# Keep-warm matmuls with start times, later expected casts and two weight loads per slot in a fused attention kernel

## The chip, the cores and the metric

The kernel runs on one core of a Trainium2 chip. The metric is the device time of one execution in microseconds (us), as a median of several executions; lower is better. The engines have short names in the profile: PE is TensorE (matmuls and transposes), ACT is ScalarE (tanh, exp), DVE is VectorE, POOL is GpSimd, SP is SyncE, which issues transfers. Each engine runs its own queue in order, and engines wait for each other through semaphores.

## The reference

Two attention blocks run one after the other. The first has 8 batches of 12 heads with 448 tokens and a head dimension of 64, and caps its scores with a tanh. The second reads the first one's output as x of 448 x 768 per batch, projects it to q, k and v of 4 experts, runs causal attention for each expert, and weighs two of the four expert outputs per token by a gate.

```python
scores = cap * np.tanh(scale * np.matmul(q, k.transpose(0, 1, 3, 2)) / cap)
attn = softmax(scores); x = np.matmul(attn, v)      # heads side by side: 8 x 448 x 768
for e in range(4):
    a = softmax(causal(scale * (x @ wq[e]) @ (x @ wk[e]).T))
    out += gate[e] * (a @ (x @ wv[e]) @ wo[e])      # gate: softmax of the top 2 of x @ w_gate
```

## The kernel before

**Pairs and slots.** The 96 heads of the first block are worked as 48 pairs, six pairs to a batch. A pair p is loaded by SP in float32 (`load`, L294), cast to float16 (`a_cast`, L376: q at L385, k at L386, the last 64 rows of k at L391, then v in `a_castv`, L397), transposed on PE and copied to SBUF by DVE (`a_tr`, L408), multiplied on PE into scores (`fill`, L470), put through tanh on ACT (`tanh`, L489, the row at L510) and exp (`expo`, L512, the row at L516), and multiplied with v on PE (`a_pv`, L575, rows L544 and L550). A last transpose (`a_xt`, L622, row L585) lays the result out as the second block's x. Pairs 0 and 1 have their q cast by DVE; from pair 2 on every cast is POOL's.

The program on ACT is fixed: a list `prog` in which each pair has a slot. The tanh of a pair comes in four parts, written here T(p,0) to T(p,3), and from pair 3 on the exp of the pair before, E(p-1), stands between T(p,0) and T(p,1). The scores live in two buffers, so the fill of one part can begin only when ACT has read the part two places earlier. The second block's exps (L781, called X) come in between for the batches that are done; X of batch 0 stands in slots 9 and 11.

**Who orders PE's queue.** A `Plan` (L17 to L129) simulates PE, DVE and ACT while the kernel is built and so decides in which order the units of work are put into PE's queue. Its clock begins at 7.0. It knows `dur` (L998): a slot without second-block exps is 0.055 + 0.373, then three times 0.055 + 0.746, then 0.08 + 0.00084 x 3136, which is 5.545. `nom["S", p]` is the nominal start of slot p, counted from 0, so `nom + 7` is the planner's own time of it. A unit has a cost, dependencies, and a due time; it is a candidate once its dependencies are in `plan.done`. `step` (L64) takes, among the candidates that can start within 0.3 of the earliest, the one with the earliest due time. `do_fill` (L1019) places each fill at the time at which its buffer is expected to be free, and lets `pump` (L85) put units into the gap before it. The planner's times set the order alone. On the chip PE takes the next instruction in the queue as soon as the semaphores allow it.

**`slot(p)` (L1046)** is called when the program reaches slot p. It drops the keep-warm units left from the slot before and offers new ones; issues the loads of pairs six slots ahead; casts the pair four slots ahead (`a_cast`) and tells the planner when to expect that cast, in `plan.done[("cast", i)]`; issues some of the second block's weight loads from POOL's queue (L1064) and tells the planner to expect them 26.0 later; and offers the transposes of pair p + 2, the products of pair p - 1, and in slots 6, 12, ... the projections of a finished batch (`batch`, L1117). A cast and a weight load that are issued in the same slot stand behind each other in POOL's queue.

**Keep-warm units** (`keep_warm`, L894) are matmuls of a zero tile, 128 x 512, into a buffer that nothing reads. They have a due time of 1.0e9, so the planner takes one only where nothing else can start within 0.3. Nine and two more are issued before the planner begins.

There are 16 weight loads: q and k of experts 0 and 1 (four), v (four), q and k of experts 2 and 3 (four), and the output weights (four), in this order.

Of the kernel before, what the change touches and what calls it, by code (L numbers as in the profile page):

```python
# [239 lines left out]
def kernel(  # L240
# [15 lines left out]
    B, H, S, Dh = q.shape  # L256
# [37 lines left out]
    def load(p, n=2):  # L294

        b, j = divmod(p, HP)
        h0, h1 = 2 * j, 2 * (j + n)
        qf = stage.tile([QP, 2 * n, QC * Dh], f32, name=f"qf_{p}", tag="qf")
        kf = stage.tile([128, 2 * n, KC * Dh], f32, name=f"kf_{p}", tag="kf")
        vf = stage.tile([128, 2 * n, KC * Dh], f32, name=f"vf_{p}", tag="vf")  # L300
        ktf = stage.tile([128, n, Dh], f32, name=f"ktf_{p}", tag="ktf")
        vtf = stage.tile([128, n, Dh], f32, name=f"vtf_{p}", tag="vtf")
        for i in range(n):
            h = slice(2 * i, 2 * i + 2)
            staged[p + i] = (qf[:, h], kf[:, h], vf[:, h], ktf[:, i], vtf[:, i])

        def rows(dst, src, c):
            return lambda eng: eng.dma_start(dst, src.rearrange("h (p c) d -> p h (c d)", c=c))

        def tails(dst, src, i):  # L310
            t = src[b, h0:h1, KM:S].rearrange("(j two) p d -> two p j d", two=2)
            return lambda eng: eng.dma_start(dst[64 * i : 64 * (i + 1)], t[i])  # L312

        return [
            rows(qf, q[b, h0:h1], QC), rows(kf, k[b, h0:h1, 0:KM], KC), tails(ktf, k, 0),
            tails(ktf, k, 1), rows(vf, v[b, h0:h1, 0:KM], KC), tails(vtf, v, 0), tails(vtf, v, 1),
        ]
# [3 lines left out]
    LOAD, CAST, TR = 6, 4, 2  # L321
    DEEP = 18

    def ahead(p, n, since, more=4):

        new = range(p + n + more * (p > since), p + n + more * (p >= since) + 1)
        return [i for i in new if i < NP]

    warm = const.tile([128, 512], f16, name="warm")
# [46 lines left out]
    def a_cast(p):  # L376
        if p >= NP:
            return
        eng = nc.vector if p < 2 else nc.gpsimd
        assert p < 8 or ("tr", p - 8) in plan.done  # L380
        assert p < 12 or ("pv", p - 12, 1) in plan.done
        qf, kf, vf, ktf, vtf = staged.pop(p)
        q16 = hd.tile([QP, QC, 2, Dh], f16, name=f"q16_{p}", tag="q16", bufs=8)
        k16 = hd.tile([128, KC, 2, Dh], f16, name=f"k16_{p}", tag="k16", bufs=8)
        eng.tensor_copy(q16, qf.rearrange("p h (c d) -> p c h d", c=QC))  # L385
        nc.gpsimd.tensor_copy(  # L386
            k16, kf.rearrange("p h (c d) -> p c h d", c=KC)
        )
        for g in range(2):
            r = slice(64 * g, 64 * (g + 1))  # L390
            eng.tensor_copy(ktz[p % 8][r, r], ktf[r, :])  # L391
        cast[p] = (q16, k16)
        vcast[p] = (vf, vtf)
        if p > 1:
            a_castv(p)
# [506 lines left out]
    plan = Plan()  # L902
# [35 lines left out]
    def b_const(i):  # L938
        if i == 0:
            nc.gpsimd.memset(ltm, 0.0)  # L940
            nc.gpsimd.affine_select(
                out=ltm, in_=ltm, compare_op=ALU.is_ge, fill=-60000.0, base=0,
                pattern=[[1, 128]], channel_multiplier=-1,
            )
        else:
            nc.vector.memset(vtL, 0.0)
            nc.vector.memset(vtL[64:128, :, Dh : Dh + 1], 1.0)
        nc.vector.memset(vtB[i], 0.0)
        nc.vector.memset(vtB[i][0:64, 0:E:2, Dh : Dh + 1], 1.0)
        nc.vector.memset(vtB[i][64:128, 1:E:2, Dh : Dh + 1], 1.0)  # L950
        for t in pB[2 * i : 2 * i + 2]:
            nc.vector.memset(t[:, 0:64], 0.0)
# [85 lines left out]
    nom = {}  # L1038
# [7 lines left out]
    def slot(p):  # L1046

        plan.work[:] = [u for u in plan.work if u["key"][0] != "warm"]
        for i in range(14 if p < 3 else 8 if p < 7 else 4 if p < 13 else 0):
            plan.add(("warm", p, i), 0.22, 0.0, [], 1.0e9, keep_warm)  # L1050
        if p % 2 == 0:
            for i in ahead(p, LOAD, DEEP):
                if i % 2 == 0:
                    for f in load(i):
                        f(nc.sync)
        for i in ahead(p, CAST, DEEP + 2):
            a_cast(i)
            plan.done[("cast", i)] = max(
                5.0 * i + 1.0, plan.act + 4.0 + 3.5 * (i - p - CAST) * (p == DEEP + 2)
            )  # L1060
        for _ in range(3 if p else 2):
            if loads:
                w, dst, src = loads.pop(0)
                nc.gpsimd.dma_start(dst, src)  # L1064
                plan.done["w", w] = plan.act + 26.0
        if p in (4, 5):
            b_const(p - 4)
        for i in (1, 2) if p == 0 else ahead(p, TR, DEEP + 4, 4):
            plan.add(("tr", i), 0.43, 0.95, [("cast", i)], nom["S", i] - 3.0, a_tr, i)
        if 1 <= p < len(UNITS):  # L1070
            u = UNITS[p - 1]
            es = [("E", u)]
            due = nom["S", p + 1] + 2.0
            if isinstance(u, tuple):
                i = "AB".index(u[1])
                u = u[0]
                plan.parts(("pv", u, i), 2, 0.47, 0.55, es, due, a_pv, u, i)
                d = [("pv", u, i)]
                plan.add(("xt", u, "AB"[i]), 0.12, 0.27, d, due, a_xt_part, u, i)
            else:  # L1080
                plan.parts(("pv", u, 0), 2, 0.47, 0.55, es, due, a_pv, u, 0)
                d = [("pv", u, 0)]
                plan.parts(("pv", u, 1), 2, 0.47, 0.55, d, due, a_pv, u, 1)
                plan.add(("xt", u), 0.22, 0.35, [("pv", u, 1)], due, a_xt, u)
        if p >= HP and p % HP == 0 and p < NP:
            batch(p // HP - 1)
        if p == NP - 1:
            last_qk()
        if p == NP:
            last_vg()  # L1090
# [6 lines left out]
    def last_qk():  # L1097
        for r in range(2):
            g = ("qk", "A", r)
            due = nom["X", B - 1, r, 0] - 2.0  # L1100
            for j in range(NDC):
                d = [x_of(j, "A"), ("w", ("q", r)), ("w", ("k", r))] + [(*g, j - 1)] * (j > 0)
                plan.add(
                    (*g, j), 0.22, 0.66 * (j == NDC - 1), d, due, qk_mm, "A", r, j,
                    aux={0: "open", NDC - 1: "close"}.get(j), group=g,
                )

    def last_vg():

        due = nom["X", B - 1, 1, 0]  # L1110
        d = [x_of(NDC - 1, "A")]
        plan.parts(("vl", 0), 4, 1.32, 0.75, d, due, lv_part)
        plan.add(("lgA",), 0.6, 0.2, d, due, l_logits)
        plan.add(("g1A",), 0.0, 1.0, [("lgA",)], due, b_gate, B - 1, "A", aux=None)
        plan.add(("gA",), 0.0, 0.8, [("g1A",), ("G", B - 1)], due, b_gate2, B - 1, "A", aux=None)

    def batch(b):  # L1117
        x = ("xt", HP * b + HP - 1)
        t0, t1 = nom["X", b, 0, 0], nom["X", b, 1, 0]
        for r, t in enumerate((t0, t1)):  # L1120
            plan.parts(("q", b, r), 3, 1.13, 0.55, [x, ("w", ("q", r))], t - 4.0, b_qk, b, r, "q")
            plan.parts(("k", b, r), 3, 1.13, 0.55, [x, ("w", ("k", r))], t - 4.0, b_qk, b, r, "k")
        for n in range(4):
            d = [("v", b, n - 1)] if n else [x, ("w", "v")]
            plan.parts(("v", b, n), 2, 0.66, 0.6, d, t0 + 2.0 * n, b_v, b, n)
        plan.add(("g1", b), 0.0, 1.0, [("v", b, 3)], t1 + 1.0, b_gate, b, aux=None)
        plan.add(("g", b), 0.0, 0.8, [("g1", b), ("G", b)], t1 + 3.0, b_gate2, b, aux=None)
        for e in range(E):
            due = t1 + 6.0 + 3.0 * e
            d = [("X", b, e // 2, 1), ("g", b)] + [("pvB", b, e - 1)] * (e % 2)  # L1130
            plan.add(("pvB", b, e), 0.31, 0.7, d, due, b_pv, b, e)
            if e % 2:
                plan.add(("oT", b, e // 2), 0.22, 0.35, [("pvB", b, e)], due, b_ot, b, e // 2)
        for n in range(4):
            for f in range(2):
                i = 2 * n + f
                d = [("oT", b, 1), ("w", "o")] if i == 0 else [("wo", b, *divmod(i - 1, 2))]
                due = t1 + 19.0 + 1.5 * i
                plan.add(("wo", b, n, f), 0.33, 0.5, d, due, b_wo, b, n, f)
# [522 lines left out]
```

## Time and profile before

| what | value |
|---|---|
| median of 5 runs | 324.2 us (323.09 to 325.06) |
| the profiled execution's own time | 324.7 us |
| span of its profile, first to last instruction | 323.0 us |
| outside the span | 1.7 us |
| ACT busy | 306.2 us, 95% of the span |
| PE busy | 287.4 us, 89% |
| DVE busy | 217.8 us, 67% |
| POOL busy (its DMA issues are not counted) | 157.2 us, 49% |
| mean granted PE clock | 0.993 |
| keep-warm matmuls in the trace | 82 |

The table is read from the profile's page and the dummy tile's rows. A busy share is an average over the whole span. What bounds a stretch is read from that stretch: the row that stood idle there, and the engine named as releaser. In a timeline row the first two numbers are the start and the length of a group of like instructions, `x7` is how many there are, and the bracket at the end is the engine's idle time just before the group with the row that ended it. Lengths of PE rows overlap, since matmuls are pipelined; the distance between starts tells more.

### The profile page before, as it was taken

The page shows a single profiled execution, that of the slowest core. Times are in us where ns is not written, and L with a number is a line of the kernel's source. Part 1 is how long each engine was busy: PE and PEld are TensorE (multiplying, and loading weights), DVE is VectorE, ACT ScalarE, POOL GpSimd, SP SyncE. Part 2 cuts the span into 40 slices and gives each one's busy share as a digit, 9 for nine tenths or more (in the row PEclk, how much of TensorE's full clock was granted, in tenths as well). Part 3 has the DMA queues.
Part 4 walks back from the last instruction along what each step waited for, and adds up shares of the span by engine and source line. Part 5 has one row for each costly group of instructions (what it writes and reads, how often), then busy time and mean ns, then how long its engine had stood idle before and what let it go on. Part 6 is the DMA issues. An engine that isn't in the chain of part 4 may idle for free.

```text
span 323.0 us, 9113 instructions
## 1 busy us (share of the span) xinstructions
PE 287.4 (89%) x3454; PEld 179.9 (56%) x3454; DVE 217.8 (67%) x760; ACT 306.2 (95%) x311; POOL 157.2 (49%) x480
## 2 busy tenths in 40 slices
PE   7879899998999789997899889997899879999991
PEld 2445556654565555665555655655565555557760
DVE  4434446776767777678766985777867975578672
ACT  3996999999999999999999999999999999999881
POOL 3639999865806389874914386082804200220200
PEclk9997999999999999999999999999999999999999
DMA  7599999990185989786073990279012102020027
GB/s 158 166 222 248 221 231 230 234 205 3 50 220 145 254 212 287 184 218 151 11 212 127 284 227 2 101 197 217 4 52 97 26 2 98 2 76 2 3 99 244
DMA packets 65404, 46.22 MB, mean 143 GB/s; under 512 B 26000, under 2 KB 61968, under 8 KB 65360
## 3 DMA queue, kind: packets, MB, share of 16 engines
q1 hardware_dynamic: 54000, 43.19, 51.9%
q0 software_dynamic: 10512, 1.58, 7.2%
q10 hardware_dynamic: 848, 0.87, 0.8%
q8 instruction: 27, 0.44, 0.6%
q14 instruction: 17, 0.14, 0.1%
HBM read 36.19 MB, written 11.01 MB: 146 GB/s over the span
## 4 chain that ended last, share of the span: by engine, by line
ACT 73%; PE 12%; issue 6%; DMA 5%; SPq 1%; DVE 1%; POOL 1%; POOLq 0%
ACT y L510 34%; ACT p L516 28%; ACT pBs L781 8%; DMA qf<-in_q_dram 4%; DMA kf<-in_k_dram 2%; PE wops L863 2%; PE vps L640 1%; PE pv L550 1%; PE dummy L898 1%; PE qkA L1163 1%; ACT pB L516 1%; SPq L312 1%; PE pv L544 1%; PE kps L724 1%; ACT yB L510 1%
## 5 line engine op out<-in xcount | busy, mean ns | idle before, releaser
L510 ACT ACTIVATE y<-s 128x896 f16<-128x896 f32 (+1 forms) x176 | 140.6, 973 | 3.2 <-PE s L480 2.7
L516 ACT ACTIVATE p<-y 128x3136 f16<-128x3136 f16 x44 | 130.7, 2970 | 0.1
L789 POOL TENSOR_SCALAR_AFFINE_SELECT pBs<-pBs 128x128 f16<-128x128 f16 (+1 forms) x112 | 28.3, 278 | 106.6 <-ACT pBs L781 104.8
L550 PE MATMUL pv<-v16s,p 128*128 128x65 f16 x1056 | 54.6, 194 | 0.0
L480 PE MATMUL s<-qt,kt 64*128 64x448 f16 x264 | 46.6, 356 | 7.8 <-ACT y L510 5.2
L550 PEld LDWEIGHTS <-p 128*128 128x128 f16 x1056 | 46.8, 98 | 3.4 <-issue 0.3
L544 PE MATMUL pv<-vtzs,p 128*128 128x130 f16 x176 | 39.5, 224 | 8.3 <-ACT p L516 6.0
L563 DVE TENSOR_TENSOR xk<-pv,rc 128x256 f16<-128x256 f32 x96 | 40.7, 424 | 3.3
L559 DVE RECIPROCAL rc<-pv 128x4 f32<-128x4 f32 x96 | 17.2, 179 | 33.2 <-PE pv L550 31.6
L370 DVE COPY ob<-wops 128x384 f32<-128x384 f32 (+1 forms) x53 | 29.3, 553 | 9.4 <-PE wops L863 9.1
L544 PEld LDWEIGHTS <-p 128*128 128x128 f16 x176 | 17.1, 97 | 27.2 <-ACT p L516 16.3
L480 PEld LDWEIGHTS <-kt 64*128 64x128 f16 x264 | 16.4, 93 | 28.2 <-issue 20.6
L781 ACT ACTIVATE pBs<-sB 128x960 f16<-128x960 f32 (+1 forms) x28 | 32.1, 1162 | 0.0
L385 POOL CAST q<-qf 112x512 f16<-112x512 f32 x46 | 28.1, 611 | 6.3 <-DMA qf<-in_q_dram 4.4
L863 PE MATMUL wops<-wo,oT 128*128 128x384 f16 x128 | 29.9, 326 | 0.3 <-ACT oT L370 0.3
L640 PE MATMUL vps<-wvg,xT 128*128 128x260 f16 (+1 forms) x192 | 29.8, 275 | 0.0
L399 POOL CAST v16s<-vf 128x384 f16<-128x384 f32 x48 | 24.3, 506 | 6.0 <-DMA vf<-in_v_dram 3.2
L370 DVE COPY xT<-xtp 128x448 f16<-128x448 f16 (+2 forms) x52 | 19.1, 368 | 11.5 <-PE xtp L585 10.1
L386 POOL CAST k<-kf 128x384 f16<-128x384 f32 x48 | 24.3, 506 | 3.9 <-DMA kf<-in_k_dram 3.9
L898 PE MATMUL dummy<-warm 128*128 128x512 f16 x82 | 24.9, 422 | 1.3 <-DVE warm L330 1.3
L404 POOL CAST vtzs<-vtf 64x64 f16<-64x64 f32 x96 | 22.6, 235 | 3.4 <-DMA vtf<-in_v_dram 0.6
L391 POOL CAST ktzs<-ktf 64x64 f16<-64x64 f32 x92 | 21.3, 232 | 2.8
(178 smaller groups left out, 527.4 us busy)
## 6 DMA issues: line engine op xcount, KB each, us to landing
qf<-in_q_dram SPq DMA_DIRECT2D x22, 448.0 KB, 6.0
out_dram<-ob SPq DMA_DIRECT2D x23, 384.0 KB, 2.5
kf<-in_k_dram SPq DMA_DIRECT2D x22, 384.0 KB, 6.8
vf<-in_v_dram SPq DMA_DIRECT2D x22, 384.0 KB, 6.0
ktf<-in_k_dram SPq DMA_DIRECT2D x44, 32.0 KB, 5.7
vtf<-in_v_dram SPq DMA_DIRECT2D x44, 32.0 KB, 5.2
out_dram<-ob SPq DMA_DIRECT2D x7, 192.0 KB, 2.8
kf<-in_k_dram SPq DMA_DIRECT2D x4, 192.0 KB, 3.3
```

The lines of the kernel that those rows point to most:

```text
L370: (nc.scalar.copy if act else nc.vector.tensor_copy)(dst, src)
L480: nc.tensor.matmul(sc[:, g, 0:S], kt[r, 128 * i : 128 * (i + 1)], qt[r, :], start=True, stop=True,)
L510: nc.scalar.activation(dst, src, AF.Tanh, scale=isc / capf)
L516: nc.scalar.activation(pt[:, 0:n], y.pop(u)[:, 0:n], AF.Exp, scale=capf)
L544: nc.tensor.matmul(pv[:, n, :, :], prob(p, w, 0, 0), vtz[p % 12], start=(n == 0), stop=False, skip_group_check=True,)
L550: nc.tensor.matmul(pv[:, n, g, :], prob(p, w, j, g), v16[p % 12][:, g, j - 1, :], start=False, stop=(j == KC), skip_group_check=True,)
L563: nc.vector.tensor_tensor(xt[p][:, 2 * i : 2 * i + 2, :, :], pv[:, :, :, 0:Dh], rc.broadcast_to((128, 2, 2, Dh)), ALU.mult,)
L640: nc.tensor.matmul(ps, xT[b][:, j, w : w + 128], wvg[:, j, 0 : ps.shape[1]], start=(j == 0 and first), stop=(j == NDC - 1), skip_group_che ...
L781: nc.scalar.activation(pb[:, o0 : o0 + n], st[b].pop(("sc", r, g))[:, 0:n], AF.Exp, scale=isc)
L789: nc.gpsimd.affine_select(out=blk, in_=blk, compare_op=ALU.is_ge, fill=0.0, base=0, pattern=[[1, n]], channel_multiplier=-1,)
L863: nc.tensor.matmul(ps, st[b]["oT", r][:, w : w + 128], wo2[r][:, f * (D // 2) : (f + 1) * (D // 2)], start=(r == 0), stop=(r == 1),)
L898: nc.tensor.matmul(dummy, warm[:, 0:128], warm, start=True, stop=True)
```

## The change

Three edits are made in `slot`, and nothing else changes.

```diff
     def slot(p):
 
         plan.work[:] = [u for u in plan.work if u["key"][0] != "warm"]
-        for i in range(14 if p < 3 else 8 if p < 7 else 4 if p < 13 else 0):
-            plan.add(("warm", p, i), 0.22, 0.0, [], 1.0e9, keep_warm)
+        n = 9 if p < 3 else 6 if p < 7 else 3 if p < 13 else 0
+        for i in range(n):
+            plan.done["from", p, i] = nom["S", p] + 7.0 + 5.6 * i / n
+            plan.add(("warm", p, i), 0.22, 0.0, [("from", p, i)], 1.0e9, keep_warm)
...
         for i in ahead(p, CAST, DEEP + 2):
             a_cast(i)
             plan.done[("cast", i)] = max(
-                5.0 * i + 1.0, plan.act + 4.0 + 3.5 * (i - p - CAST) * (p == DEEP + 2)
-            )
-        for _ in range(3 if p else 2):
+                5.65 * i + 1.5 if i < 12 else 0.0,
+                plan.act + 4.0 + 3.5 * (i - p - CAST) * (p == DEEP + 2),
+            )
+        for _ in range(2):
             if loads:
                 w, dst, src = loads.pop(0)
                 nc.gpsimd.dma_start(dst, src)
                 plan.done["w", w] = plan.act + 26.0
```

First, fewer keep-warm units are offered (9, 6 and 3 in a slot in place of 14, 8 and 4), and each has a time before which the planner doesn't take it, spread evenly over 5.6 from the slot's start. Second, the planner expects the cast of pair i at 5.65 i + 1.5 in place of 5.0 i + 1.0 up to pair 11; from pair 12 on only the second term counts. Third, every slot issues at most two weight loads, so the 16 loads take slots 0 to 7 in place of 0 to 5.

## The prediction

> **What bounds the kernel now.** I read the page first, then ACT's waits, then ACT's, PE's and POOL's timelines around the longest wait, then a table of windows.
>
> The page, busy tenths in 40 slices of 8.1 us:
>
> ```profile
> PE   7879899998999789997899889997899879999991
> ACT  3996999999999999999999999999999999999881
> PEclk9997999999999999999999999999999999999999
> ```
>
> ACT is full from the second slice to the 37th, but for the fourth. There the granted PE clock also has its only dip. ACT's waits by releaser:
>
> ```profile
> ACT kt L370 <- PE tpsk L421: 2.8, 1, 2.8
> ACT y L510 <- PE s L480: 2.7, 1, 2.7
> ACT ob L370 <- PE wops L863: 2.4, 2, 1.9
> ```
>
> The first is the start (6.15 us), the third the end (after 305); neither place is edited. The second is one wait of 2.7 us. ACT around it:
>
> ```profile
> 24.64 1.75 ACT L510 ACTIVATE y<-s 128x896 f16<-128x896 f32 x2
> 29.11 1.35 ACT L510 ACTIVATE y<-s 128x896 f16<-128x896 f32 x2 [2.71 <-PE s L480]
> ```
>
> By its place in the program this is T(3,3), late by 2.71 us. PE's queue before it:
>
> ```profile
> 22.02 0.37 PE L414 MATMUL tps<-ident,q 112*128 112x112 f16 x4 [0.30 <-POOL q L385]
> 23.70 0.23 PE L419 MATMUL tps<-ident,ktzs 128*128 128x128 f16 x1 [1.30 <-POOL ktzs L391]
> 24.02 0.55 PE L480 MATMUL s<-qt,kt 64*128 64x448 f16 x4
> ...
> 24.74 3.03 PE L898 MATMUL dummy<-warm 128*128 128x512 f16 x7
> 27.56 0.32 PE L544 MATMUL pv<-vtzs,p 128*128 128x130 f16 x1
> ...
> 28.70 0.36 PE L480 MATMUL s<-qt,kt 64*128 64x448 f16 x2
> ```
>
> PE takes up the transposes of pair 4 at 22.02 and stands until 23.70 for POOL's cast. Then come seven dummies, the products of pair 2, one more dummy, and only then the fill that ACT wants. The windows (columns: us, then busy time and count of PE, PEld, DVE, ACT, POOL; granted clock; DMA share; GB/s):
>
> ```profile
> 21.50:24.90 3.40, 1.80 (x24) 0.99 (x22) 1.38 (x5) 3.40 (x4) 1.96 (x6) 1.00 1.02 255
> 24.90:28.30 3.40, 3.40 (x20) 1.65 (x18) 0.41 (x2) 1.50 (x2) 3.24 (x8) 0.50 1.15 257
> 260.40:263.80 3.40, 2.16 (x29) 1.43 (x29) 3.03 (x12) 3.40 (x6) 0.00 (x0) 1.00 0.00 0
> ```
>
> After the thin stretch at 21.5 the clock is halved for one stretch of 3.4 us. A stretch with PE busy for 2.16 kept it.
>
> **Where the 2.71 come from.** Later, at full clock, eight dummies begin 1.89 us from first start to last end, and one alone takes 0.38: (1.89 - 0.38) / 7 = 0.216 apart. Seven are 1.51; here they took 27.56 - 24.74 = 2.82. The products took 28.39 - 27.56 = 0.83, and 0.50 at 33.22. The eighth dummy took 0.31, not 0.22. The clock so accounts for 1.31 + 0.33 + 0.09 = 1.7, and the stand with the dummies behind it for the other 1.0.
>
> **Part by part.**
>
> *Expected casts.* The planner took pair 4's cast for done at 5 x 4 + 1 = 21.0. E(2) stands at 21.35 in its clock (slot 3 is 7 + 2.83 + 2 x 5.545 = 20.92, and T(3,0) is 0.43) and at 21.94 in the trace, so the trace's clock is 0.6 later there. The cast ended in the trace at 23.12 + 0.52 = 23.64, that is 23.0 for the planner: two late. After the change it is expected at 5.65 x 4 + 1.5 = 24.1. By hand, the planner then puts the fills of T(3,1) and T(3,2) first (21.2 to 21.9), the output transposes of pair 1, four dummies that its start times allow (20.92, 21.85, 22.79, 23.72), pair 4's transposes at 24.1, pair 2's first products to 25.0, and the fill of T(3,3) at 25.01. On the chip: the cast is there at 23.64, the transposes end near 24.1; the products wait for E(2), to about 24.8, and end near 25.3; the fill's buffer is free when T(3,1) ends, 24.64 + 0.81 = 25.45; with the 0.41 from fill to ACT it is ready at 25.9. T(3,2) ends at 24.64 + 1.75 = 26.39 at the latest. The wait is gone, 2.7 us, with 0.4 to spare: **-2.7**. If the clock were halved all the same, the products (0.83) would end at 25.7 and the fill (about 0.7) at 26.4: a rest of 0.4. Bounds: 0 and -2.71; taken is the whole, since the rows leave room.
>
> What is late next? Pairs 5 to 11 are expected 0.105 later each relative to their slots (5.65 against 5.545). Pair 6's transposes move behind the dummies of slot 5: planned 35.4, copied by DVE at 37.2, wanted by T(6,0) at 37.6. For pairs 7 to 9 the planner's margin is slightly negative (-0.1 to -0.3). On the chip it isn't: POOL's casts of pair 5 ended at 28.5 and went on 5.0 apart, so PE finds them done and doesn't wait for the planned minute. By the 0.43 of the transposes and 0.95 of DVE's copies, pair 9 is ready near 53.4, wanted near 54.9. Cost taken: 0; bounds 0 to 0.3 in each of slots 7 to 9, so 0.9.
>
> *Keep-warm units.* In slots 0 to 2 the ones offered nearly cover the ones taken (two fewer in slot 0). In slot 3 four or five stand where one stood in the thin stretch: 1.80 + 3 x 0.22 is about 2.5 busy, above the 2.16 that kept the clock. In slots 4 to 6 five are taken in place of eight: 0.65 us less in 5.55. The stretch there with the fewest, 38.6 to 42.0, had PE busy for 3.07; if all three were lost in it 2.4 remain. Cost taken: 0, as PE has waits there; bounds -0.2 (less in front of a fill) and, per lost stretch, the 1.7 above.
>
> [...]
>
> *Two weight loads.* A load holds POOL's queue for 0.83 us. Slots 1 to 4 have issued three; with two, casts of pairs 6 to 9 come up to 2.5 us sooner, and the same loads delay pairs 10 to 13, which then end where they did, at 61.7. As ACT is 2.7 ahead, POOL's masks of batch 0 (first at 61.97, behind those casts) are no longer immediate, but their reader stands in PE's queue near 64. Cost 0, cover 2.
>
> The delicate place is the q and k weights of experts 2 and 3. Before, the last q load went at 41.16 and landed 17.8 us later, 58.9; PE used it at 60.23. Now it goes near 46.8, and PE comes to it near 59.5: the planner holds it back to 32.0 + 26 = 58.0 and places it at 58.75. The loads of that queue landed 1.3 to 3.3 us apart from 38.7 on whatever their spacing at issue, with four or more outstanding, so I expect the same landing, 58.9: cost 0. With the least, median and greatest latency of the loads issued after 38 us (13.0, 16.0, 17.8) it would land at 59.8, 62.8 or 64.6: PE would stand 0.3, 3.3 or 5.1 us, and ACT, with 0.4 of room, lose 0, 2.9 or 4.7.
>
> From slot 13 on no edit reaches the planner's inputs but through its state. ACT had no wait there from 29.11 to 305, so everything should move forward by the same 2.7.
>
> **Sum.** 324.7 - 2.7 = **322.0** against the profiled execution's own time. The median before is 324.2, 0.5 less; its fastest run, 323.09, is what my division gives without the halved clock (324.7 - 1.7 = 323.0), so I take the runs to differ in that wait, and 322.0 for the median too. Its own range is 321.2 to 322.6.
>
> **Rivals.**
> 1. *A part of the wait stays*: cast 4 depends on a DMA landing (k at 22.6), or the clock still falls. 0.4 to 1.7 remain: 322.4 to 323.7. For it: 0.4 of room only, one profile. Against: the dummies now lie where PE stood. Chance 0.18.
> 2. *The wait moves to the weights* in slot 9, landing at 62.8: -2.7 + 2.9, 324.9, no change. For it: latency grew to 17.8 with load. Against: the landings are paced by the queue. Chance 0.08. The end (PE and ACT after 290) reordered for the worse by 1 to 2 us gives the same time: 0.04.
> 3. *Slower: the same weights land later still.* From a landing past about 64.0 on, a loss of 4.3 or more puts it over 325.8; at 64.6 it is 326.7. Chance 0.10.
>
> **Numbers.** The forecast has 0.60. I call 0.5% (1.6 us) what a measurement of this kernel can tell from no change: faster is below 322.6, slower above 325.8. Faster: the forecast, 0.60 (what of it lies above that line, rival 1 makes up below it). Same: rivals 1 and 2, 0.30. Slower: rival 3, 0.10. The range leaves out rival 3 and the worst of 2: 321.1 to 324.6.
>
> **What the profile after would show.** Right: no ACT wait for s L480 near 26; four or five dummies between 22 and 23.7 and pair 4's transposes after them without a stand over 0.3 us; clock 1.00 through 40 us; ACT's last exp of a pair ending near 302.4, not 305.1. Wrong: a PE wait for a wq or wk landing near 60; a clock of 0.50 in slots 3 to 8; DVE's copies of pairs 6 to 9 followed by an ACT wait; or rows equal up to 290 and a longer end.

## The result and the profile after

| what | before | after |
|---|---|---|
| median | 325.13 us (79 runs, 323.09 to 329.37) | 326.72 us (44 runs, 324.14 to 330.04) |
| the profiled execution's own time | 324.7 us | 325.82 us |
| span of its profile | 323.0 us | 324.1 us |
| mean granted PE clock in the profile | 0.993 | 0.989 |
| keep-warm matmuls in the trace | 82 | 67 |

The ratio after to before is 1.0046, with a 95% interval of 1.0032 to 1.0060: slower by 1.0 to 2.0 us. That is just inside the 0.5% that the prediction called no change, and it lies 4.7 us above the forecast of 322.0 and above the whole range. Here and below, medians and ranges are of all runs, while ratios leave out the few slow ones, over 1.5% above the fastest run of their kernel.

The page of after, busy tenths in 40 slices of 8.1 us:

```profile
ACT  3999996999999999999999999999999999999882
PEclk9999999999999989999999999999999999999997
```

ACT's hole has moved, from the fourth slice to the seventh (48.6 to 56.7 us), and the clock's dip from the fourth (0.50 from 24.91 to 28.32) to the 15th (0.50 from 118.78 to 122.20; the 7 in the last slice lies behind ACT's work). ACT's longest waits, and PE's waits for a DMA:

```profile
ACT y L510 <- PE s L476: 4.1, 3, 3.0
ACT kt L370 <- PE tpsk L421: 2.9, 1, 2.9
ACT ob L370 <- PE wops L863: 2.4, 2, 1.9
```

```profile
PE vps L640 <- DMA wvg<-in_moe_wv_dram: 2.8, 1, 2.8
```

The wait of 2.7 for L480 is gone. In its place stands one of 3.0 for a fill at L476, and PE now waits 2.8 for the v weights (`wvg`), a row that the profile before doesn't have. First the place that was to be mended, PE's queue in slot 3 of after:

```profile
21.94 0.62 PE L480 MATMUL s<-qt,kt 64*128 64x448 f16 x4
...
22.73 1.03 PE L898 MATMUL dummy<-warm 128*128 128x512 f16 x4
23.59 0.36 PE L414 MATMUL tps<-ident,q 112*128 112x112 f16 x4
...
25.71 0.36 PE L480 MATMUL s<-qt,kt 64*128 64x448 f16 x2
```

The order is the one that the prediction worked out by hand: fills, four dummies, pair 4's transposes without a long stand, pair 2's products, and the fill of T(3,3) at 25.71 in place of 28.70. Then PE's queue in slots 7 and 8 of after, and behind it ACT's T(8,0), which waits for the row at 52.16:

```profile
48.51 0.54 PE L724 MATMUL qps<-xT,wq 128*128 128x448 f16 x2
51.82 0.51 PE L640 MATMUL vps<-wvg,xT 128*128 128x260 f16 x3 [2.77 <-DMA wvg<-in_moe_wv_dram]
52.16 0.35 PE L476 MATMUL s<-qt,kt 128*128 128x448 f16 x1
```

```profile
52.55 0.54 ACT L510 ACTIVATE y<-s 128x448 f16<-128x448 f32 x1 [3.03 <-PE s L476]
```

And the same place of before:

```profile
48.56 0.92 PE L724 MATMUL qps<-xT,wq 128*128 128x448 f16 x4
...
51.52 0.35 PE L476 MATMUL s<-qt,kt 128*128 128x448 f16 x1
...
54.39 0.83 PE L640 MATMUL vps<-wvg,xT 128*128 128x260 f16 x6
```

The last v load, its issue and then its row in the list of issues (KB and us to landing), before:

```profile
36.12 0.85 POOL L1064 DMA_DIRECT2D wvg<-in_moe_wv_dram  x1
```

```profile
wvg<-in_moe_wv_dram POOLq DMA_DIRECT2D x1, 96.0 KB, 13.9
```

And after:

```profile
39.15 0.83 POOL L1067 DMA_DIRECT2D wvg<-in_moe_wv_dram  x1
```

```profile
wvg<-in_moe_wv_dram POOLq DMA_DIRECT2D x1, 96.0 KB, 12.6
```

Before, PE first put all of q and k of batch 0 through and came to the v products at 54.39; the last v load had landed at 50.07. After, three v products stand between q's first part and the fill of T(8,0). PE reaches them at 48.9, the last v load lands at 51.77, and the fill behind them, which has nothing to do with the weights, comes 3.03 us late for ACT.

The spans add up: -2.71 (slot 3) + 3.03 (slot 8) + 0.64 (a wait of ACT at 121.96, at the end of the stretch at 0.50 from 118.78 on) + 0.14 (the first tanh begins at 7.33, before at 7.19) = +1.10, and 324.1 - 323.0 = 1.1.

**Why the v products come so early.** Working the planner through on paper, which needs only the kernel's text, gives this. It puts the first v product at 50.93 in before and at 48.28 in after. The reason is the edit of the expected casts alone: the transposes of pairs 7 and 8 are expected later and move back in the queue. Pair 7's now stand in front of pair 5's products, and the last output transpose that batch 0 lacks (`xT` of pair 5) is put at 45.41 in place of 44.34. Pair 8's now stand between it and the first part of batch 0's q, which is put at 47.91 in place of 45.31. So the gap in front of T(8,0)'s fill, which q's third part filled before, is now filled by the first v products. For the planner the v weights are there: the last v load is issued in slot 3 and expected 26.0 later, at 46.92. In the trace it landed at 51.77; the trace's clock is some 0.9 later than the planner's there, so it came 4 us later than planned. In before the same constant was off by more (expected at 41.4, landed at 50.07), but no product stood near enough to feel it.

### The profile page after: what moved, and what is told of

Read it like the earlier page. It is cut to its first block, busy times and chain, and to the rows that moved or that the text cites. A ratio compares the mean times of both kernels' runs of the same rounds, so it can differ in the third digit from the quotient of the medians.

```text
span 324.1 us, 9086 instructions
## 1 busy us (share of the span) xinstructions
PE 284.1 (88%) x3439; PEld 179.2 (55%) x3439; DVE 215.8 (67%) x760; ACT 306.4 (95%) x311; POOL 157.2 (48%) x480
## 4 chain that ended last, share of the span: by engine, by line
ACT 66%; PE 15%; issue 6%; DMA 6%; POOL 4%; DVE 1%; SPq 0%; POOLq 0%
ACT y L510 31%; ACT p L516 25%; ACT pBs L781 8%; DMA wvg<-in_moe_wv_dram 4%; PE wops L863 2%; PE vps L640 2%; DMA vf<-in_v_dram 2%; PE pv L550 1%; PE dummy L898 1%; PE qkA L1166 1%; ACT pB L516 1%; PE pv L544 1%; PE sB L762 1%; POOL v16s L399 1%; PE s L480 1%
## 5 line engine op out<-in xcount | busy, mean ns | idle before, releaser
L510 ACT ACTIVATE y<-s 128x896 f16<-128x896 f32 (+1 forms) x176 | 138.5, 934 | 4.2 <-PE s L476 4.1
L516 ACT ACTIVATE p<-y 128x3136 f16<-128x3136 f16 x44 | 128.8, 2928 | 0.1
L550 PE MATMUL pv<-v16s,p 128*128 128x65 f16 x1056 | 56.3, 194 | 0.0
L480 PE MATMUL s<-qt,kt 64*128 64x448 f16 x264 | 46.8, 358 | 9.7 <-ACT y L510 7.1
L550 PEld LDWEIGHTS <-p 128*128 128x128 f16 x1056 | 47.6, 98 | 3.9 <-issue 0.4
L544 PEld LDWEIGHTS <-p 128*128 128x128 f16 x176 | 17.1, 97 | 28.8 <-ACT p L516 15.8
L480 PEld LDWEIGHTS <-kt 64*128 64x128 f16 x264 | 16.1, 93 | 29.5 <-issue 22.9
L781 ACT ACTIVATE pBs<-sB 128x960 f16<-128x960 f32 (+1 forms) x28 | 30.6, 1110 | 0.0
L898 PE MATMUL dummy<-warm 128*128 128x512 f16 x67 | 21.9, 414 | 1.3 <-DVE warm L330 1.3
```

Of the source, the lines that this page charges most:

```text
L480: nc.tensor.matmul(sc[:, g, 0:S], kt[r, 128 * i : 128 * (i + 1)], qt[r, :], start=True, stop=True,)
L510: nc.scalar.activation(dst, src, AF.Tanh, scale=isc / capf)
L516: nc.scalar.activation(pt[:, 0:n], y.pop(u)[:, 0:n], AF.Exp, scale=capf)
L544: nc.tensor.matmul(pv[:, n, :, :], prob(p, w, 0, 0), vtz[p % 12], start=(n == 0), stop=False, skip_group_check=True,)
L550: nc.tensor.matmul(pv[:, n, g, :], prob(p, w, j, g), v16[p % 12][:, g, j - 1, :], start=False, stop=(j == KC), skip_group_check=True,)
L781: nc.scalar.activation(pb[:, o0 : o0 + n], st[b].pop(("sc", r, g))[:, 0:n], AF.Exp, scale=isc)
```

## The experiments

My theory A was this: all of the loss is the v weights, so with v expected later the change keeps its gain. Rival B: the thinner keep-warm matmuls cost clock (0.985 as a mean over the runs of after, 0.992 over those of before), and the stand for v (PE idle until the load lands) is only a part. Rival C: the two-load edit alone is to blame, since it sends the v loads out 3 us later.

**e1, the changed kernel with the weights expected later.**

```diff
-                plan.done["w", w] = plan.act + 26.0
+                plan.done["w", w] = plan.act + 31.0
```

> The changed kernel, but the planner expects each weight load 31.0 after its issue in place of 26.0; nothing else. Theory A (the changed kernel lost its gain to PE standing 2.77 us in front of the v weights, which landed at 51.77 while PE came at 48.9): the first v product moves from 48.3 to 53.7 of the planner's clock, about 54.5 of the trace's, behind the landing; the ACT wait of 3.03 us in slot 8 goes, the span is near 321 and the median 3 us under the changed kernel's 326.7, near 323.7, a ratio to before of 0.995. Rival B (what costs is the clock, which the fewer keep-warm matmuls let fall more often): the wait may go, but mean clocks stay near 0.985 and the median stays above 325.5, ratio 1.001 or more.

Measured: 322.60 us (321.89 to 323.29) against 324.55 of before; ratio 0.9937 (0.9912 to 0.9962). PE in slots 7 and 8 of e1:

```profile
48.52 0.54 PE L724 MATMUL qps<-xT,wq 128*128 128x448 f16 x2
48.90 0.38 PE L898 MATMUL dummy<-warm 128*128 128x512 f16 x1
49.12 0.35 PE L476 MATMUL s<-qt,kt 128*128 128x448 f16 x1
...
54.16 0.50 PE L640 MATMUL vps<-wvg,xT 128*128 128x260 f16 x3
```

A dummy takes the place of the v products, the fill goes at 49.12 in place of 52.16, and ACT has no wait at slot 8. One constant turns the change from +0.46% to -0.63%. A is carried; all three edits are still in e1, so the other two cost little. The median is 1.1 us below what A gave (323.7), which took only ACT's wait off; e9 to e12 are about the rest.

**e2, the expected casts alone** (before with the second edit only).

> The kernel before with the second edit alone: later expected casts, three weight loads per slot, old keep-warm units. Theory A: the 2.71 us wait in slot 3 goes; the planner puts the first v product at 48.3 here too, and with three loads per slot the v weights land near 50.1, so PE stands about 1.2 us and ACT waits about 1.4 in slot 8; the sum is -1.3, ratio 0.996. Rival B: the keep-warm units are the old ones, so all of the wait removed is gained unless the weights take it; ratio 0.992 to 0.996 and clocks no lower than before's.

Measured: 326.42 us (324.47 to 329.83); ratio 1.0057 (1.0021 to 1.0093). The expectation was missed: the edit that was to bring the gain loses by itself. The wait in slot 3 is gone in e2 too, but PE waits for weights twice:

```profile
PE qps L724 <- DMA wq<-in_moe_wq_dram: 1.6, 1, 1.6
PE vps L640 <- DMA wvg<-in_moe_wv_dram: 0.8, 1, 0.8
```

ACT loses 1.07 at 50.65 and 1.43 at 62.60 by them. C falls: with three loads per slot v lands at 49.87, and PE is there before it all the same.

**e3, the two weight loads alone** (before with the third edit only).

> The kernel before with the third edit alone: two weight loads per slot. Both theories: the 2.71 us wait in slot 3 stays, and the first v product stays at 50.9 of the planner's clock, some 54.4 of the trace's, behind a landing near 51.8, so nothing waits for weights: ratio 1.000, within 0.3%. If it is slower by 0.5%, the loads cost in a way that neither theory has.

Measured: 323.49 us (322.51 to 326.17); ratio 0.9968 (0.9940 to 0.9997). The wait in slot 3 is there (2.94 in its profile), and PE waits for no weight, though v lands at 50.72. Alone the edit costs nothing; why it is slightly faster, if it is, the profile doesn't show.

**e4, the keep-warm matmuls alone** (before with the first edit only).

> The kernel before with the first edit alone: fewer keep-warm units with start times. Theory A: four dummies in place of seven stand before the late fill of slot 3, so its wait shortens by 0.6 to 1.2 us and nothing else moves: ratio 0.997. Rival B: clocks fall more often, the mean clock is about 0.005 lower than in before's runs and the time longer by one or two lost stretches of some 0.7 to 1.7 us: ratio 1.003 to 1.008.

Measured: 324.38 us (322.81 to 326.66); ratio 1.0006 (0.9975 to 1.0037), and a mean clock of 0.992 as before. In its profile the wait in slot 3 is 0.36, since fewer dummies stand behind the transposes and the clock wasn't halved there (1.00 from 24.9 to 28.3, behind 3.40 us with PE busy for 1.85). But the next pairs have the same fault of order, a little later. PE and ACT around slot 6 of e4:

```profile
38.07 0.37 PE L414 MATMUL tps<-ident,q 112*128 112x112 f16 x4 [0.60 <-POOL q L385]
38.99 0.23 PE L419 MATMUL tps<-ident,ktzs 128*128 128x128 f16 x1 [0.55 <-POOL ktzs L391]
```

```profile
39.83 0.54 ACT L510 ACTIVATE y<-s 128x448 f16<-128x448 f32 x1 [1.16 <-PE s L476]
```

PE stands for POOL's cast again, in front of the fill of T(6,0). Without the later expected casts the wait moves; with them it goes.

**e5, the changed kernel with 28.0 in place of 26.0.** For the planner this moves the v products alone (to 53.66) and leaves the q and k weights of the later experts where they are.

> The changed kernel with the weights expected 28.0 after issue in place of 26.0: by the planner's arithmetic this moves the v products of batch 0 (first from 48.3 to 53.7) and leaves the q product of experts 2 and 3 at 60.0, so the v weights are the one wait taken away. Theory A: as e1 was, 322.6, ratio 0.994. If the q weights of experts 2 and 3 (landing 59.8 to 61.3, reached near 60.9) also cost in most executions, it stays 0.5 us or more above e1.

Measured: 322.42 us (322.23 to 322.95) against 324.70; ratio 0.9917 (0.9887 to 0.9948). No wait of ACT longer than 0.1 us between 8 and 304 us. So it is v, not q and k, that costs.

**e6, e1 with the old keep-warm units.**

> e1 with the old keep-warm units (14, 8, 4 and no start times). Theory A (with the weight wait gone the fewer keep-warm units cost nothing on ACT): 322.6 as e1, within 0.3%, whatever the clock. Rival B (the thinned units cost): faster than e1 by 0.5 us or more, 322.1 or less, with a mean clock of 0.992 as before's.

Measured: 321.61 us (321.25 to 323.14); ratio 0.9900 (0.9863 to 0.9938), the fastest of all, with a mean clock of 0.993. These are the numbers that were given for rival B, though e1 ran on another chip. Against e5, on the same chip, it is 0.8 lower, and the intervals overlap. The profiled executions differ by nearly as much (322.23 and 321.54), but not where the dummies stand: neither has a wait of ACT over 0.1 us between 8 and 304 us, the last copy to the output ends at 314.80 in e5 and at 314.71 in e6, and behind it, where the output is stored, e5 takes 5.72 and e6 5.01. So these two executions show no cost of the thinner keep-warm; whether it has a part in the difference of the medians isn't settled.

**e7, the expected casts alone, with 38.0** (e2 with the weights expected much later, three loads a slot, old keep-warm).

> e2 (casts alone, three loads per slot, old keep-warm) with the weights expected 38.0 after issue: the v products move to 53.6 and the q product of experts 2 and 3 from 54.4 to 60.0 of the planner's clock, behind both landings. Theory A: both DMA waits of PE that e2 showed (0.8 and 1.6 us) go, and the casts' whole gain shows: 322.5, ratio 0.994. If the two-load edit is needed besides, it stays above 323.5.

Measured: 322.31 us (321.84 to 322.44); ratio 0.9910 (0.9875 to 0.9944), and PE waits for no DMA of the weights. The gain is that of the expected casts and a true landing time; the two-load edit isn't needed for it.

**e8, the changed kernel with the old keep-warm units, 26.0 kept.**

> The changed kernel with the first edit undone (old keep-warm units), weights still expected 26.0 after issue: the first v product stays at 48.3. Theory A: PE's stand of 2.8 us for the v weights and ACT's wait of 3 us stay, 326.6 within 0.5 us. Rival B (the keep-warm edit carries the loss): 325.0 or less and mean clocks of 0.990 or more.

Measured: 327.36 us (323.36 to 330.64); ratio 1.0052 (1.0013 to 1.0090), mean clock 0.984. The median is 0.3 above the range given for A. In the profiled execution (324.66) the stand is 1.83 and ACT's wait at T(8,0) 2.09, both shorter than expected. All the dummies are back and neither the loss nor the low clock goes. B falls.

**e9, e10: the stand filled with dummies.** In e9 ten dummies stand in front of the first v product of batch 0; e10 is the changed kernel beside it on the same chip.

```diff
         if n == 0 and i == 0:
             b_v_new(b)
+            if b == 0:
+                keep_warm(10)
```

> The changed kernel with ten more keep-warm matmuls right in front of the first v product of batch 0, where PE stands for the v weights anyway (ten are about 2.2 us of the 2.8). Theory A with a second term (the stand leaves PE so thin that the clock is halved after it in most executions, and the median pays about 1 us for that on top of the 3.0 us wait): mean clock rises by about 0.005 from 0.985 and the median falls from e10's by 0.7 to 1.3 us. If the wait for the weights is all there is, clock and median stay as e10's within 0.4 us, or worsen where the weights land earlier than the dummies end.

> The changed kernel once more, on the same chip as e9: near 326.6 with a mean clock near 0.985. Its profile shows another execution: theory A expects PE's stand in front of the first v product, between 1.5 and 4 us with the landing, and where the stand fills most of one 3.4 us stretch, a granted clock of 0.50 just behind it.

Measured: 325.23 us for e9 (323.85 to 326.88; ratio 1.0011, 0.9985 to 1.0038; mean clock 0.991) and 326.88 for e10 (323.22 to 328.30; ratio 1.0033, 0.9999 to 1.0067; mean clock 0.986). The dummies on PE in e9, and T(8,0) on ACT:

```profile
48.33 2.32 PE L900 MATMUL dummy<-warm 128*128 128x512 f16 x10
```

```profile
51.24 0.54 ACT L510 ACTIVATE y<-s 128x448 f16<-128x448 f32 x1 [2.26 <-PE s L476]
```

ACT's wait stays (2.26), since the dummies only fill the time until the landing at 50.43. The median is 1.65 below e10's (0.7 by the ratios, whose intervals overlap) and the clock is back. That fits a part of the loss being the halved clock behind the stand; by the times alone it isn't shown. The profiled execution of e10, at 328.19 among its longest, had the v load at 52.90, a stand of 4.16, just beyond what was expected, and a wait of 4.68 at T(8,0). The stretch of the stand had PE busy for 0.30 us, and the clock was 0.50 in the next.

**e11, e12: the changed kernel twice more, one execution each**, to see how the stand and the clock go together.

> A further profile of the changed kernel, to see how the stand for the v weights and the clock behind it vary from execution to execution: the time should be about 322.4 (e5) plus ACT's wait in slots 8 and 9, so that executions at 326 to 327 show about 4 us of ACT waits there, with the clock at 0.50 between 50 and 60 us.

> As e11: one more execution of the changed kernel; ACT's waits in slots 8 and 9, added to 322.4, should give its time within 0.7 us.

Measured: 326.12 and 327.22 us. The v loads landed at 50.66 and 52.38, PE stood 1.85 and 3.72, and ACT lost 2.40 and 3.98 at T(8,0), then 0.81 and 0.95 more at one place in the slot behind, and 0.16 at the next. The sum that was expected gives 325.8 and 327.5, both within its 0.7. e10 has the same waits in that slot (0.82 and 0.16); after, e8 and e9, whose clock stayed up there, have none. The windows, with the columns of the prediction's table, first e11, then e12, then the profiled execution of after:

```profile
47.56:50.97 3.41, 1.55 (x19) 0.78 (x17) 1.30 (x5) 1.77 (x3) 3.18 (x9) 1.00 1.63 224
50.97:54.38 3.41, 3.41 (x25) 1.53 (x23) 0.00 (x0) 2.65 (x2) 3.24 (x9) 0.50 1.36 233
```

```profile
49.90:53.31 3.41, 0.89 (x6) 0.50 (x6) 0.00 (x0) 0.15 (x1) 3.18 (x9) 1.00 1.37 250
53.31:56.72 3.41, 3.41 (x23) 1.69 (x23) 0.90 (x3) 3.41 (x3) 3.13 (x11) 0.50 1.47 212
```

```profile
47.11:50.52 3.41, 1.89 (x26) 1.15 (x26) 1.30 (x5) 2.41 (x3) 3.28 (x7) 1.00 1.65 242
50.52:53.93 3.41, 2.11 (x22) 1.16 (x23) 0.00 (x0) 1.38 (x2) 3.21 (x9) 1.00 1.34 196
```

In e11 and e12 the stand falls mostly into one stretch, which is thin (1.55 and 0.89 busy), and the next one has half the clock. In the profiled execution of after the stand of 2.77 was divided over two stretches, with 1.89 and 2.11 busy, and the clock stayed at 1.00.

**A closing sum.** e5's profiled execution takes 322.23 with no wait of ACT between 8 and 304 us and a first tanh at 7.25. Adding the waits of ACT over 0.1 us in another trace, and the difference of its first tanh, gives 322.23 + 3.67 + 0.08 = 325.98 for after (measured 325.82), 322.23 + 4.03 - 0.10 = 326.16 for e11 (326.12), 322.23 + 5.09 - 0.26 = 327.06 for e12 (327.22), 322.23 + 2.60 - 0.24 = 324.59 for e8 (324.66) and 322.23 + 2.71 - 0.06 = 324.88 for before (324.70). ACT's waits account for each of these to 0.2 us. Of the other traces, e2, e3, e4, e7, e9 and e10 come out within 0.25; e1 is 0.5 longer than its sum and e6 0.8 shorter, most of that in e6 behind the last copy to the output.

## Why the prediction was wrong

- **What bounds the kernel: right.** ACT, and one wait at T(3,3).
- **Expected casts, -2.7: right in mechanism, and in size for the profiled execution.** The order came as worked out, the wait went whole, and ACT waits for no late cast in slots 7 to 9. Where the weights are out of the way, the median gains 1.95 (e1) and 2.3 us (e5); the 2.71 is that of one execution whose clock was halved (0.50 from 24.91 to 28.32). But the planner answers a change of one expected time with another order everywhere, and the prediction followed it to the transposes of pairs 6 to 9 and not to what takes the gaps that they leave.
- **Keep-warm units, 0: right where it was argued.** The windows of slot 3 show PE busy for 2.85 and 3.03 of 3.40 (the prediction said about 2.5), those of slots 4 to 6 for 2.49 or more, all at full clock. As the whole change goes, e8 says that the dummies have no part in the loss; e6 leaves open up to 0.8 us, which its profile doesn't place there.
- **Two weight loads, 0: the step that failed**, with its sentence "The delicate place is the q and k weights of experts 2 and 3". I asked of four loads alone when they land and when they are used. In after the last q load landed at 61.30, not at 58.9 as expected, and cost nothing; by the planner's arithmetic its product stands at 60.0, not at the 58.75 that I worked out. Of v I asked neither, which put its cost at nothing without a reason; PE stood 2.77 us for it and ACT waited 3.03. Three things met there: the planner put the first v product 2.65 earlier (the expected casts), the whole time line was 2.71 earlier (the gain itself), and the landing came 1.70 later (the two loads: 51.77 against 50.07). The trace of before had the numbers for two of the three: landing 50.07, first use 54.39, a cover (the time between them) of 4.3, of which 2.7 + 1.7 = 4.4 use all. The third, the new place in front of a fill, makes the rest cost in full. The later landing isn't needed for a loss: in e2 the first two alone make PE stand 0.82 for v, and ACT wait 1.07.
- **Rival 2 had the right mechanism in the wrong place.** The wait did move to the weights, but to v at T(8,0), not to q in slot 9. Its price, 2.9, is near what the profiled execution paid (3.03), but by luck: it was worked out for another load. Across executions it was 2.4 to 4.7, and some 1.0 to 1.1 more behind the stand where the clock was halved, which the rival didn't price although the wait in slot 3 had just shown the same pair, a stand (1.30 us) and then a halved clock (0.50). I gave it 0.08; the loads of v would have deserved most of rival 3's 0.10 too.
- **The range** ended at 324.6, below rival 2 by its own sum (324.9) and without any clock term: too narrow by that. Its start was low too: 324.2 from five runs, where 79 runs have 325.13. Rival 3's two numbers have two starts, 4.3 on 321.5 and 4.7 on 322.0; on 322.0, 3.8 would have done.

## What to carry to other kernels

An edit that pulls a time line forward uses up the cover of every transfer behind it: list landing and first use of each load, subtract the gain and the later issue, and look at the smallest rest first. A constant in a planner that is wrong (here 26.0, for loads that landed 4 to 8 us after it) can be harmless until the order changes, and then it costs in full where the unit stands in front of work that the bound engine waits for. After changing an expected time, follow the planner's new order to its end and not only the unit that was to move; and count the clock behind a stand as a part of its price (in e11 and e12 ACT waited 0.97 and 1.11 us in the slot behind it).

## What the runs showed of the hardware

- **The halved stretches lasted 3.413 us and began whole multiples of that apart.** The clock was 0.50 in before from 24.91 to 28.32 and again from 321.87 (87 stretches later), in after from 118.78 to 122.20 and again from 320.17 (59 stretches); in e3 the halved ones began at 24.60, 113.35 and 225.99 (26 and 33 stretches). Laid end to end from a halved one, stretches of this length at full clock number 86 in before and 86 in after, up to 300 us. Two of the 172 were followed by a halved one: PE was busy for 1.81 us in the one (before, from 21.49) and for 2.10 in the other (after, from 115.37). Of the rest the thinnest had 1.89, 2.11 and 2.16 (after, from 47.10, 50.52 and 183.64), each with 1.00 in the next. So busy time alone doesn't part the two kinds here. The longer stand wasn't the one with the halved clock behind it: 1.85 us in e11, mostly in one stretch, left 1.55 busy, with 0.50 in the next; 2.77 us in after, divided over two, left 1.89 and 2.11, with 1.00 behind both.
- **Stretches with mostly transposes kept the full clock.** In after PE was busy for 2.70 us from 146.09 to 149.50, and only 0.81 of that were other matmuls (`sB` and `s`, 146.38 to 147.19); the clock was 1.00 there and up to 152.91. In e8 there is a stretch in which all but 0.36 us of PE's busy 1.95 are transposes. Those 0.36 alone are less than the 0.89 and 1.55 of e12 and e11, yet the clock was 1.00 in it and in the next:

```profile
145.05:148.46 3.41, 1.95 (x32) 1.67 (x34) 3.31 (x16) 3.41 (x3) 0.00 (x0) 1.00 1.13 241
```

- **GpSimd's q, k and v weight loads mostly landed some 2.5 us apart, though issued 0.8 to 3.9 apart.** In before the loads of 96 KB that landed from 38.75 to 61.62 came 1.3 to 3.3 us apart, though they were issued 0.8 to 3.4 apart; in after it was 2.4 to 2.8 up to 57.02, and then 4.3 to the last q load. The last v load, issued 3.0 us later in after than in before (39.15 and 36.12), landed 1.7 later; over four traces of the changed kernel it came at 50.66, 51.77, 52.38 and 52.90.
- **The kernels with a stand had the wider spread.** e5, with none, has runs from 322.23 to 322.95, and e1 from 321.89 to 323.29. Over more runs the changed kernel, with e10's, has 323.22 to 330.04, and before, whose stand is in slot 3, 323.09 to 329.37. That the landing and the place of the 3.413 us stretches together make this spread fits the four traces of the changed kernel; it is the author's reading, and no run shows it by itself.
